# Backward chain: the gradient of the heads' output by 32 rows as weights in four column groups, and dV from it token by token

## Chip, cores and metric

The kernel runs on one core of a Trainium2 chip. The metric is the device time of one execution in microseconds (us). TensorE is the matrix engine: a matmul has a stationary operand (the weights, up to 128x128) and a moving one whose columns stream through; a result with 32 weight columns uses a quarter of the array's columns, and four such column groups can work side by side. VectorE, ScalarE and GpSimd (POOL) copy and calculate; transfers are issued from queues, here those of SyncE (SP) and POOL.

## The reference

A pre-norm block of memory attention followed by a gated FFN, forward and backward. The output and nine gradients are wanted: of x, the start memory, Wq, Wk, Wv, Wo and the three FFN weights.

```python
B, S, Dm = (1, 2048, 448);  H, Dh = (16, 256);  M, seg = (8, 32)
...
mem = mem0
for s in range(n_seg):                      # 64 segments, one after another
    xs = x[:, s * seg_len:(s + 1) * seg_len, :]
    h = concatenate([mem, xs], axis=1)      # 40 rows
    q, k, v = h @ Wq, h @ Wk, h @ Wv        # by head
    p = softmax(where(mask, q @ k.T * scale, -1e9))
    o = (p @ v) @ Wo
    mem = o[:, :M, :]                       # 8 rows to the next segment
    outs.append(o[:, M:, :])
...
h = x + A(layernorm(x));  out = h + swiglu(layernorm(h))
```

The backward pass runs through the segments from 63 to 0. For a segment, with dO the gradient of `o` (40 rows): dOh = dO Wo^T by head, dV = P^T dOh, dP = dOh V^T, dS from the softmax, dQ = dS K, dK = dS^T Q, and the gradient of the 40 input rows is the sum of dV Wv^T, dK Wk^T and dQ Wq^T. Its 8 memory rows belong to dO of the segment before.

## The kernel before

The stages follow one another: the forward chain over 64 segments, the FFN forward and backward over eight pairs of row tiles, the backward chain over 64 segments, then a tail of weight gradients. A tile is four segments (128 rows). All engines' instructions are put in a fixed order when the program is built, by a planner that goes by priorities and its own estimates of durations; what stands in `k.prio.crit()` comes first, in the order of the program text, and other work is put where the planner sees an engine free. `tc.issue_after(x)` puts instructions behind x on their engine. PSUM buffers: `ps1` five, `fx1` two, `po1` one, each a bank of 128 x 2 KB. `evac` copies PSUM to SBUF, on VectorE ("v", L75) or ScalarE ("s", L76).

In SBUF a segment's 40 rows are kept with the 8 memory rows last: columns 0:32 are the segment's own x rows, 32:40 the memory rows. So of the 40 columns the last 32 (`M:L`) hold the 24 output rows and the 8 rows that come from the chain, and the first 8 (`0:M`) hang on no other segment.

One segment s of `backward_chain` (r = s % 4 is its place in its tile t; r goes 3, 2, 1, 0):

- `load_seg` (L1155), for s - 1 while s runs: V from `VG` by a DMA transpose (`load_v`, L1153), Q and K rows from `T1` and `T0q`/`T0k` (L1163, eight loads), all on SP; P from `P_all` on POOL (L1166), from which POOL makes the block-diagonal P_bd of two heads (L1168).
- dOh (L1236): 32 blocks of 128 head columns, each with four parts of the 448 rows of Wo^T; the weights are 128x128 of `WoT_sb`, the 40 columns of `do_roll` are moving: 128 matmuls into four PSUM tiles, copied to `doT` (L75/L76).
- `token_major` (L1245): 16 transposes of `doT` into `dO_sb`, two copies.
- dP (L1254): 32 matmuls of doT and V; then VectorE's chain L1261, L1263, L1264 and L1267, which gives dS_bd.
- `heads("v")` (`head_mm`, L1213): 16 matmuls of dO_sb with P_bd, copied into `blk["v"]` (own rows) and `lo["v"]` (first 8 rows) by ScalarE; `rows_in("v")` (L1293) multiplies 32 rows of each block by Wv^T in four column groups into `pH`.
- `heads("k")`, the turn of dS (L1304, 16 matmuls) with two copies, 12 of K's rows, `heads("q")`, the other 20 of K's rows and 32 of Q's.
- The copy of `pH` to `omb` (L1319), the fp32 matmuls that add the four groups and turn the result (L1322), and VectorE's copy of the 8 memory rows to `do_roll` (L1326), at which the next segment starts.
- At r = 0, not in `crit()`: the first 8 rows of four segments against all three weights (L1378, 96 matmuls), their turn (L1385), the tile's input gradient (L1393) and its layer norm.

`prep_tile` (L1147, L1150) brings 128 rows of the FFN's input gradient `DHb` turned into `do_roll`. The first segment's work is fed by three generator steps inside the last FFN pair, which load Wo^T, Wv^T, Wk^T and Wq^T (3 to 3.6 MB each) where FFN weights lay.

The forward chain has in `qk_rows` (L569, L576) a product in which 32 rows are the weights and 512 columns move, in four column groups, with the last 64 of 448 rows done as two row groups side by side. On SP it stores q and k rows (L824) and V (L826) of each segment.

## Time and profile before

| what | us |
|---|---|
| median of 3 runs | 2935.48 |
| the runs | 2923.96 to 2941.26 |
| the profiled execution | 2921.87 |
| its span | 2920.1 |
| forward chain, about | 40 to 950 |
| FFN, about | 950 to 1257 |
| backward chain | 1257 to 2262 |
| tail | from there to the end |
| TensorE busy in 1281 to 2250 (969 us) | 959.21 |
| VectorE, ScalarE, POOL busy there | 505.20, 372.12, 226.39 |
| share of DMA time there | 0.54 |

In the profile's lines PE is TensorE's matmuls and PEld its weight loads, DVE VectorE, ACT ScalarE; a group is line, engine, operation, output and inputs, shapes, count, busy time, mean duration of one in ns, and idle time before it. The chain of waits gives pieces in order: start, length, engine and line. "issue" is time in which an engine waited for nothing that the profile shows. SPq is SP's queue, with the time that issuing took.

### The profile page before, as it was taken

To read this page: it belongs to the slowest core of one execution; us is meant where nothing else is said; L and a number is where in the kernel's file an instruction comes from. 1 tells how busy PE (TensorE), PEld (TensorE's weight loads), DVE (VectorE), ACT (ScalarE), POOL (GpSimd) and SP (SyncE) were. 2 spreads that over 40 slices of the span, in tenths; PEclk is the share of its full clock that TensorE was granted. 3 is DMA by queue.
4 is the path that set the end of the run, shared out by engine and by line. 5 is a ranking of instruction groups with operands and counts; after the bars stand their busy time and mean duration, and the time that the engine had idled before them with its cause. 6 is when DMAs were issued, how large, how long until landed. Compare 5 with 4: busy or idle time off the path is not lost.

```text
span 2920.1 us, 108265 instructions
## 1 busy us (share of the span) xinstructions
PE 2805.9 (96%) x47650; PEld 1746.3 (60%) x47650; DVE 1328.6 (45%) x3320; ACT 1077.0 (37%) x2590; POOL 704.1 (24%) x1676
## 2 busy tenths in 40 slices
PE   4999999999999999989999999999999989999998
PEld 3555565555555555667777777677766544545444
DVE  4555565556455666745555555555554011111110
ACT  2554454455454454433333333343333011111110
POOL 1222232233222222422222222222222111212211
PEclk9999999999999999999999999999999999999999
DMA  7577777777778988985555555555555998969941
GB/s 258 152 193 192 192 193 195 192 194 200 198 185 229 285 219 215 257 259 151 142 145 154 144 141 155 137 148 149 142 154 170 347 269 175 207 183 238 207 147 52
DMA packets 743132, 552.14 MB, mean 189 GB/s; under 512 B 601796, under 2 KB 639060, under 8 KB 740100
## 3 DMA queue, kind: packets, MB, share of 16 engines
q1 hardware_dynamic: 692788, 402.38, 55.9%
q0 software_dynamic: 49872, 142.83, 14.4%
q8 instruction: 374, 6.13, 0.9%
q14 instruction: 98, 0.80, 0.1%
HBM read 169.84 MB, written 236.13 MB: 139 GB/s over the span
## 4 chain that ended last, share of the span: by engine, by line
PE 80%; issue 8%; DMA 4%; ACT 3%; DVE 2%; POOL 2%; SPq 0%; POOLq 0%; ACTq 0%; DVEq 0%
PE po L1293 11%; PE psf L1487 8%; PE psf L1236 7%; PE psf L569 6%; PE psf L704 5%; PE psf L1213 5%; PE psf L967 4%; PE po L751 4%; PE fx L1378 3%; PE fx L1487 3%; PE fx L1091 3%; PE psf L593 2%; PE psf L1322 2%; PE psf L1245 2%; PE psf L485 2%
## 5 line engine op out<-in xcount | busy, mean ns | idle before, releaser
L76 ACT CAST arA<-psf 128x384 bf16<-128x384 f32 (+6 forms) x1083 | 419.8, 428 | 845.0 <-PE psf L1487 215.1
L75 DVE CAST arA<-psf 128x256 bf16<-128x256 f32 (+6 forms) x797 | 358.4, 471 | 687.8 <-PE psf L1487 248.9
L1293 PE MATMUL po<-arW,arA 128*32 128x448 bf16 x6144 | 328.1, 355 | 5.6 <-DMA arW<-Tq 4.1
L1487 PEld LDWEIGHTS <-arA 128*128 128x128 bf16 x1440 | 139.0, 98 | 160.6 <-issue 4.8
L1236 PEld LDWEIGHTS <-arW 128*128 128x128 bf16 x8192 | 211.2, 96 | 23.3 <-issue 18.4
L1487 PE MATMUL psf<-arW,arA 128*128 128x512 bf16 x882 | 222.7, 381 | 0.0
L1293 PEld LDWEIGHTS <-arA 128*32 128x32 bf16 x6144 | 146.8, 96 | 120.3 <-ACT arA L76 9.3
L1236 PE MATMUL psf<-arA,arW 128*128 128x40 bf16 x8192 | 217.2, 180 | 0.8 <-DVE arA L1326 0.8
L704 PE MATMUL psf<-arW,arA 128*64 128x512 bf16 x1536 | 212.1, 382 | 0.0
L569 PE MATMUL psf<-arW,arA 128*32 128x512 bf16 x3072 | 189.8, 381 | 7.7 <-DVE arA L75 0.9
L76 ACT COPY arA<-psf 128x512 bf16<-128x512 bf16 (+3 forms) x206 | 142.9, 727 | 39.5 <-PE psf L593 24.0
L76 ACT CAST arB<-psf 128x64 bf16<-128x64 f32 (+1 forms) x320 | 107.7, 337 | 135.1 <-PE psf L576 73.6
L967 PE MATMUL psf<-arW 128*128 128x256 bf16 (+1 forms) x1288 | 149.0, 277 | 5.0 <-DVE arA L75 3.7
L75 DVE COPY arA<-psf 128x512 bf16<-128x512 bf16 (+2 forms) x204 | 104.3, 512 | 99.5 <-PE psf L1245 82.4
L967 PEld LDWEIGHTS <-arW 128*128 128x128 bf16 (+1 forms) x1344 | 103.2, 97 | 56.9 <-issue 45.4
L569 PEld LDWEIGHTS <-arA 128*32 128x32 bf16 x3072 | 70.3, 96 | 105.1 <-issue 28.8
L751 PE MATMUL po<-arW,arA 128*32 128x256 bf16 (+1 forms) x4096 | 126.9, 261 | 1.2 <-DVE arA L75 1.2
L1564 POOL DMA_DIRECT2D out_dram<-arA x96 | 52.2, 544 | 262.0 <-DVE arA L75 233.6
L1527 PE MATMUL psf<-arW 128*128 128x448 bf16 x525 | 111.6, 352 | 3.0 <-DVE arA L75 1.6
L1213 PEld LDWEIGHTS <-arW 128*128 128x128 bf16 x2048 | 79.5, 99 | 49.6 <-issue 48.1
L751 PEld LDWEIGHTS <-arA 128*32 128x32 bf16 x4096 | 104.0, 96 | 8.5 <-DVE arA L75 1.5
L1168 POOL COPY arB<-arB 40x320 bf16<-40x320 bf16 x128 | 58.9, 460 | 174.8 <-DMA arB<-P_all 86.7
(298 smaller groups left out, 4553.5 us busy)
## 6 DMA issues: line engine op xcount, KB each, us to landing
arW<-T SPq DMA_DIRECT2D x256, 128.0 KB
X_o<-arA SPq DMA_DIRECT2D x37, 512.0 KB
T<-arA SPq DMA_DIRECT2D x64, 256.0 KB
X_v<-arA POOLq DMA_DIRECT2D x30, 512.0 KB, 4.9
X_k<-arA POOLq DMA_DIRECT2D x30, 512.0 KB, 4.7
X_q<-arA POOLq DMA_DIRECT2D x30, 512.0 KB, 4.1
out_dram<-arA POOLq DMA_DIRECT2D x84, 128.0 KB, 3.8
VG<-arA SPq DMA_DIRECT2D x64, 160.0 KB
```

The lines of the kernel that those rows point to most:

```text
L75: return nc.vector.tensor_copy(out=out, in_=in_)
L76: return nc.scalar.copy(out=out, in_=in_)
L569: nc.tensor.matmul(banks[b][w][32 * q:32 * q + 32, :], lhsT=hT_roll[:, kc, sl, M:L], rhs=(Wq_sb, Wk_sb)[w][:, kc, col(q, b)], start=(b == ...
L704: nc.tensor.matmul(pV[b][64 * g:64 * g + 64, 0:512], lhsT=hT_flat[:, kc, sl * L:sl * L + 64], rhs=Wv_sb[:, kc, n * 512:(n + 1) * 512], sta ...
L751: last = nc.tensor.matmul(pO[32 * q:32 * q + 32, 0:w], lhsT=xblk[:, j, r * SEG:(r + 1) * SEG], rhs=Wo_sb[:, cj(j), 256 * dh:256 * dh + w], ...
L967: nc.tensor.matmul(ps[fp][:, f2 * 256:(f2 + 1) * 256], lhsT=Wt[lo:hi, kc, c * P:(c + 1) * P], rhs=xT[lo:hi, kc, :], start=(kc == 0 and f2 ...
L1091: k.last_dh = nc.tensor.matmul(pdh[:, 0:D], lhsT=srcT[:, tt, c, :], rhs=WT[:, c, :], start=(i == 0), stop=(i == 2 * FC - 1))
L1213: nc.tensor.matmul(ps[b][:, i * 2 * L:(i + 1) * 2 * L], lhsT=lhs[:, at, :], rhs=rhs_bd[:, cl // 2, :, :].rearrange("p g n -> p (g n)"), st ...
L1236: nc.tensor.matmul(pss[b][:, jj * L:(jj + 1) * L], lhsT=WoT_sb[:, kc, c * P:(c + 1) * P], rhs=do_roll[:, kc, sl, :], start=(kc == 0), stop ...
L1293: nc.tensor.matmul(pH[32 * (j % 4):32 * (j % 4) + 32, 0:D], lhsT=blk[nm][:, j, r * SEG:(r + 1) * SEG], rhs=WT[:, cj(j), :], start=(nm == " ...
L1487: k.last_mm = nc.tensor.matmul(pa[i][:, 0:w], lhsT=lhs_of(b)[:, i // 2 * P:(i // 2 + 1) * P], rhs=rhs_of(q, b, i % 2), start=(b == 0), sto ...
L1527: k.last_mm = nc.tensor.matmul(pa[i][:, 0:D], lhsT=lhs_of(b, i), rhs=rhs_of(b), start=(bi == 0), stop=(bi == m + 3))
```

## The change

dOh of a segment is split by rows. The 32 rows `M:L` become the weights: for each part of the 448 rows, four column groups of 32 take four different 1024-column quarters of Wo^T, 512 columns at a time (`grads_by_col`: 12 matmuls for bank 0, eight for the last 64 of the 448 rows in two row groups, 12 for bank 1). The result lies token by token (`dO_own`: partitions are 4 quarters x 32 rows). Four transposes for each bank (`grads_turned`) give the columns `M:L` of `doT` for dP.

The first 8 rows of four segments together are also 32 rows. They are made for the tile t - 1 in two halves in the segments r = 1 and r = 0 of tile t (for the first tile before the chain begins), stored to a new DRAM tensor `RO` by SP, and loaded again segment by segment (`load_rest`); turned, they lie in `R4_b`, from which POOL copies 8 columns into `doT` each segment.

dV is then made from the token-major rows without another transpose: `value_own`, eight matmuls of `dO_own` with P of four heads laid block-diagonally (`P4`, 160 columns), and `value_rest`, eight with 32 weight rows from `dOr` and `P4r`, into the same three PSUM tiles. P4 is loaded by four DMAs on SP (`load_p`), P4r from a new tensor `PR` that the forward chain fills by four stores a segment, after one store of zeros over all of it at s = 0.

The order changes as well: dP begins with the heads whose half is turned; the turn of dS comes before the k heads; all of K's rows come behind the q heads. A pad of 64 columns of `DHb` and `omb` holds a copy of the last 64 columns instead of zeros, since the weights of the last 64 rows lie twice, on both halves of the partitions. Removed are 16 transposes and the 16 head matmuls of dV per segment.

```diff
+              RO=dt("RO", [NT, P, 1024]), PR=dt("PR", [NSEG, 4 * M, 16 * L]),
...
+            blank = A(20, 2560)
+            nc.gpsimd.memset(blank, 0.0)
+            nc.sync.dma_start(out=dr["PR"].rearrange("s q n -> (s q n)").rearrange("(p a n) -> p a n", p=P, n=2560),
+                              in_=blank.unsqueeze(1).to_broadcast([P, 4, 2560]))
...
+        pr = dr["PR"][s].rearrange("(q k) (i c n) -> q k i c n", q=4, i=4, c=4)
+        for q in range(4):
+            g, x = divmod(q, 2)
+            nc.sync.dma_start(out=pr[q, :, :, 2 * x + g, :], in_=P_sb[64 * g:64 * g + M, 4 * x:4 * x + 4, :])
...
+            nc.gpsimd.tensor_copy(out=dh_b[:, D:DP], in_=dh_b[:, D - 64:D])
...
-    WoT_sb = W(0, KC, HD)
+    WoT_sb, Wo3 = W(0, KC - 1, HD), W(24, 2048)
+    dO_own, dOr, P4r = W(28, 2, 512), W(30, 3, P), W(30.75, 4, 4, L)
...
-    dO_sb = A(52, 16, P)
-    doT = A(56, 32, 64)
+    R4_b, hRo = [A(52 + 2 * i, 32, 4 * M) for i in range(2)], B(4.75, KC, 4 * M)
+    doT_flat = A(56, 32 * L + 24)
+    doT = doT_flat[:, 0:32 * L].rearrange("p (c n) -> p c n", n=L)
+    P4 = A(58.5625, 4, 4, L)
...
+        nc.gpsimd.tensor_copy(out=hRo.rearrange("p k (g j) -> p k g j", j=M), in_=do_roll[:, :, s0:s0 + 4, 0:M])
+
+    def grads_by_col(lhs, banks, part, alone=False):
+        last = None
+        if part in ("h", "h0", "h1"):
+            for q in range(4):
+                for b in (0, 1) if part == "h" else (int(part[1]),):
+                    nc.tensor.matmul(banks[b][32 * q:32 * q + 32, :], lhsT=lhs(KC - 1)[64 * b:64 * b + 64], rhs=Wo3[64 * b:64 * b + 64, 512 * q:512 * q + 512],
+                                     start=(part == "h" and b == 1), stop=(part != "h" or b == 0), skip_group_check=True)
+        else:
+            for kc in range(KC - 1):
+                for q in range(4):
+                    c0 = 1024 * q + 512 * part
+                    last = nc.tensor.matmul(banks[part][32 * q:32 * q + 32, :], lhsT=lhs(kc), rhs=WoT_sb[:, kc, c0:c0 + 512],
+                                            start=(kc == 0 and (part == 0 or alone)), stop=(part == 1 and not alone and kc == KC - 2), skip_group_check=True)
+        return last
+
+    def grads_out(banks, b):
+        k.evac(dO_own[:, b, :], banks[b][:], "vs"[b])
+
+    def grads_turned(pt, dst, b):
+        for i in range(4):
+            last = nc.tensor.transpose(pt[:, 512 * b + i * P:512 * b + (i + 1) * P], dO_own[:, b, i * P:(i + 1) * P], ident[:, :])
+        k.evac(dst.rearrange("p (x c) n -> p x c n", x=2)[:, :, 8 * b:8 * b + 8, :],
+               pt[:, 512 * b:512 * b + 512].rearrange("p (c x n) -> p x c n", x=2, n=32), "v")
+        return last
+
+    def rest_rows_saved(t, b):
+        nc.sync.dma_start(out=dr["RO"][t][:, 512 * b:512 * b + 512], in_=dO_own[:, b, :])
+
+    def load_rest(s):
+        t, r = divmod(s, 4)
+        src = dr["RO"][t].rearrange("(q r k) (m e) -> r q k m e", q=4, k=M, e=P)
+        for w in range(3):
+            n = (3, 3, 2)[w]
+            nc.sync.dma_start(out=dOr[32 * w:32 * w + 32, 0:n], in_=src[r][:, :, 3 * w:3 * w + n])
+            nc.sync.dma_start(out=P4r[32 * w:32 * w + 32].rearrange("p i c n -> p (i c n)"), in_=dr["PR"][s])
+
+    def load_p(s):
+        pa = dr["P_all"][s].rearrange("p (x i n) -> p x i n", x=2, n=L)
+        for q in range(4):
+            g, x = divmod(q, 2)
+            nc.sync.dma_start(out=P4[32 * q:32 * q + 32, :, 2 * x + g, :], in_=pa[64 * g + M:64 * g + L, x])
 
     def load_v(s):
         return nc.sync.dma_start_transpose(out=vT, in_=dr["VG"][s])
 
     def load_seg(s):
+        load_p(s)
         if s < NSEG - 1:
+            load_rest(s)
             load_v(s)
...
+    def rest_lhs(kc):
+        return hRo[:, kc, :]
+    with k.prio.crit():
+        banks = [k.ps1(), k.ps1()]
+        for part in (0, "h", 1):
+            grads_by_col(rest_lhs, banks, part)
+        pt = k.ps1()[:].bitcast(BF16)
+        for b in range(2):
+            grads_out(banks, b)
+            grads_turned(pt, R4_b[(NT - 1) % 2], b)
+            rest_rows_saved(NT - 1, b)
+        load_rest(NSEG - 1)
...
+    def v_bank(ps, b):
+        n = (3, 3, 2)[b]
+        return 3 * b, n, ps[b][:, 0:4 * L * n]
+
+    def v_out(ps, m):
+        return v_bank(ps, m // 3)[2].rearrange("p (x m n) -> p x m n", x=2, n=2 * L)[:, :, m % 3]
+
+    def p_rows(rhs, m):
+        return rhs[:, m // 2].rearrange("p (x g) n -> p x (g n)", x=2)
+
+    def value_rest(ps):
+        for m in (0, 3, 6, 1, 4, 7, 2, 5):
+            w, a = divmod(m, 3)
+            nc.tensor.matmul(v_out(ps, m), lhsT=dOr[32 * w:32 * w + 32, a, :], rhs=p_rows(P4r[32 * w:32 * w + 32], m),
+                             start=(a == 0), stop=False, skip_group_check=True)
+
+    def value_own(ps, m0, m1):
+        for m in range(m0, m1):
+            nc.tensor.matmul(v_out(ps, m), lhsT=dO_own[:, m // 4, m % 4 * P:(m % 4 + 1) * P], rhs=p_rows(P4, m),
+                             start=False, stop=True, skip_group_check=True)
+
+    def v_rows(ps, b):
+        m0, n, bank = v_bank(ps, b)
+        return slice(2 * m0, 2 * m0 + 2 * n), bank.rearrange("p (x c n) -> p x c n", x=2, n=L)
...
-            pss = [k.ps1() for _ in range(4)]
-            for j in range(MC):
-                c = cj(j)
-                b, jj = divmod(j, 8)
-                for kc in range(KC):
-                    with tc.issue_after(k.last_dh.ins) if s == NSEG - 1 and j == 0 and kc == 0 else nullcontext():
-                        nc.tensor.matmul(pss[b][:, jj * L:(jj + 1) * L], lhsT=WoT_sb[:, kc, c * P:(c + 1) * P],
-                                         rhs=do_roll[:, kc, sl, :], start=(kc == 0), stop=(kc == KC - 1))
-            for b in range(4):
-                k.evac(doT[:, 8 * b:8 * b + 8, 0:L], pss[b][:, 0:8 * L].rearrange("p (c n) -> p c n", n=L), "vsvs"[b])
-
-            def token_major(hf):
-                ph = k.ps1()[:].bitcast(BF16)
-                for i in range(8):
-                    c0 = 2 * (8 * hf + i)
-                    nc.tensor.transpose(ph[:, i * P:(i + 1) * P], doT[:, c0:c0 + 2, :].rearrange("p c n -> p (c n)"), ident[:, :])
-                k.evac(dO_sb[:, 8 * hf:8 * hf + 8, :], ph.rearrange("p (c n) -> p c n", n=P), "sv"[hf])
-            token_major(0)
-            token_major(1)
+            def own_lhs(kc):
+                return do_roll[:, kc, sl, M:L]
+            banks = [k.ps1(), k.ps1()]
+            for part in (0, "h", 1):
+                with tc.issue_after(k.last_dh.ins) if s == NSEG - 1 and part == 0 else nullcontext():
+                    grads_by_col(own_lhs, banks, part)
+            grads_out(banks, 0)
+            grads_out(banks, 1)
+            nc.gpsimd.tensor_copy(out=doT[:, :, 0:M], in_=R4_b[t % 2][:, :, r * M:(r + 1) * M])
+            pV = [k.ps1() for _ in range(3)]
+            value_rest(pV)
+            pt = k.ps1()[:].bitcast(BF16)
+            grads_turned(pt, doT[:, :, M:L], 0)
+            value_own(pV, 0, 4)
+            grads_turned(pt, doT[:, :, M:L], 1)
             pD = k.ps1()
-            for h in range(8):
-                for g in range(2):
-                    for dc in range(DC):
-                        j = 2 * (2 * h + dc) + g
-                        nc.tensor.matmul(pD[64 * g:64 * g + 64, h * L:(h + 1) * L], lhsT=doT[:, j, :], rhs=vT[:, 2 * h + dc, L * g:L * g + L],
-                                         start=(dc == 0), stop=(dc == DC - 1), skip_group_check=True)
+            ready = [(0, 0), (0, 1), (1, 0), (4, 0), (4, 1), (5, 0), (1, 1), (5, 1)]
+            for h, g in ready + [(h, g) for h in (2, 3, 6, 7) for g in range(2)]:
+                for dc in range(DC):
+                    j = 2 * (2 * h + dc) + g
+                    last_d = nc.tensor.matmul(pD[64 * g:64 * g + 64, h * L:(h + 1) * L], lhsT=doT_flat[:, j * L:j * L + 64], rhs=vT[:, 2 * h + dc, L * g:L * g + L],
+                                              start=(dc == 0), stop=(dc == DC - 1), skip_group_check=True)
+            with tc.issue_after(last_d.ins):
+                value_own(pV, 4, 8)
...
-            heads("v", dO_sb, P_bd)
+            def rows_in(nm, WT, js):
+                for j in js:
+                    last = nc.tensor.matmul(pH[32 * (j % 4):32 * (j % 4) + 32, 0:D], lhsT=blk[nm][:, j, r * SEG:(r + 1) * SEG],
+                                            rhs=WT[:, cj(j), :], start=(nm == "v" and j < 4), stop=(nm == "q" and j >= MC - 4),
+                                            skip_group_check=True)
+                return last
+            for b in range(3):
+                js, v = v_rows(pV, b)
+                k.evac(blk["v"].rearrange("p (x c) n -> p x c n", x=2)[:, :, js, r * SEG:(r + 1) * SEG], v[:, :, :, M:L], "s")
+            if s == 0:
+                k.tl.outs(7, 9, 0, 6)
             score_grads()
-            first_rows("v")
-            rows_in("v", WvT_sb, 0, MC)
-            heads("k", Q_sb, dS_bd)
+            for b in range(3):
+                js, v = v_rows(pV, b)
+                k.evac(lo["v"].rearrange("p (x c) n -> p x c n", x=2)[:, :, js, r * M:(r + 1) * M], v[:, :, :, 0:M], "s")
+            with tc.issue_after(last_d.ins):
+                last_v = rows_in("v", WvT_sb, [16 * x + j for a, e in ((0, 6), (6, 12), (12, 16)) for x in range(2) for j in range(a, e)])
+            if r < 2 and t > 0:
+                rest_bank = [k.ps1()] * 2
+                with tc.issue_after(last_v.ins):
+                    for part in ((1, "h1") if r == 0 else (0, "h0")):
+                        grads_by_col(rest_lhs, rest_bank, part, True)
             pT = [k.ps1(), k.ps1()]
             for h in range(8):
                 for g in range(2):
...
             for g in range(2):
                 turned["vs"[g]] = k.evac(dST_bd[64 * g:64 * g + L, :, g, :],
                                          pT[g][64 * g:64 * g + L, 0:8 * L].rearrange("p (h n) -> p h n", n=L), "vs"[g])
+            with tc.issue_after(last_t.ins):
+                heads("k", Q_sb, dS_bd)
+            if r < 2 and t > 0:
+                with tc.issue_after(turned["sv"[r]].ins):
+                    grads_out(rest_bank, 1 - r)
+                rest_rows_saved(t - 1, 1 - r)
             with tc.issue_after(turned["v"].ins):
                 own_rows("k", 2, "v")
             first_rows("k", turned)
-            with tc.issue_after(last_t.ins):
-                rows_in("k", WkT_sb, 0, 12)
-            heads("q", K_sb, dST_bd)
-            rows_in("k", WkT_sb, 12, MC)
-            rows_in("q", WqT_sb, 0, MC)
+            last_q = heads("q", K_sb, dST_bd)
+            with tc.issue_after(last_q.ins):
+                rows_in("k", WkT_sb, range(MC))
+            if r < 2 and t > 0:
+                grads_turned(k.ps1()[:].bitcast(BF16), R4_b[(t - 1) % 2], 1 - r)
+            rows_in("q", WqT_sb, range(MC))
             first_rows("q", turned)
             k.last_om = nc.vector.tensor_copy(out=om[:, 0:D], in_=pH[:, 0:D])
+            nc.vector.tensor_copy(out=om[:, D:DP], in_=pH[:, D - 64:D])
```

## The prediction

> **What bounds the kernel now.** I read the page first (busy shares, slices, the chain's shares), then the chain of waits and the timeline of single segments of the backward chain, then the same for the forward chain and the hand-over. From the page:

> ```profile
> span 2920.1 us, 108265 instructions
> PE 2805.9 (96%) x47650; PEld 1746.3 (60%) x47650; DVE 1328.6 (45%) x3320; ACT 1077.0 (37%) x2590; POOL 704.1 (24%) x1676
> PE 80%; issue 8%; DMA 4%; ACT 3%; DVE 2%; POOL 2%; SPq 0%; POOLq 0%; ACTq 0%; DVEq 0%
> L1236 PE MATMUL psf<-arA,arW 128*128 128x40 bf16 x8192 | 217.2, 180 | 0.8 <-DVE arA L1326 0.8
> ```

> TensorE is busy nearly everywhere, so what counts is how long it issues, and where a serial chain holds it. The output gradient by head is L1236, 128 matmuls a segment. One ordinary segment in the chain of waits (start, length, what):

> ```profile
> 1618.03 3.30 PE psf L1236 x128
> 1621.33 1.00 PE psf L1245 x16
> 1622.33 0.62 PE psf L1254 x32
> 1622.95 0.74 PE psf L1213 x16
> 1623.69 0.30 PE fx L1378 x4
> 1624.00 1.60 PE po L1293 x32
> 1625.60 0.01 issue
> 1625.61 0.73 PE psf L1213 x16
> 1626.35 0.30 PE psf L1304 x16
> 1626.65 0.74 PE po L1293 x12
> 1627.39 0.68 PE psf L1213 x16
> 1628.07 2.57 PE po L1293 x52
> 1630.64 0.75 PE fx L1378 x13
> 1631.39 1.06 PE psf L1322 x8
> 1632.45 0.49 PE fx L1378 x6
> ```

> The segment takes 14.91 us and TensorE never rests. L1378 (first rows of the last tile) is filler put where TensorE would wait: for the VectorE chain behind dP (1623.00 to 1625.61), and for the copies around the fp32 turn L1322. Three segments of a tile take 14.9; the one that also has L1385 and L1393 takes 17.2 (1571.05 to 1588.25). Sixteen tiles at (3 x 14.9 + 17.2) = 61.9 us are the 980 us of the backward chain.

> The price of the new form is in the forward chain, where 32 rows are already weights in column groups:

> ```profile
> 705.78 1.48 PE psf L569 x24
> 707.26 0.56 PE psf L576 x16
> 707.82 1.41 PE psf L569 x24
> ```

> **The change, part by part.**

> *From the start of a segment to dP.* Before: 3.30 + 1.00 + 0.62, and VectorE starts on dP 4.97 us after the segment began. After: part 0 is 12 matmuls of 512 columns, 12/24 of 1.41 = 0.71; the halves are 8, 0.28 to 0.34 (half of 0.56, with 0.05 for the change of form); part 1 another 0.71. The sum is 1.76, and L569's single time of 0.38 against 0.06 per issue leaves about 0.17 of tail. Bank 0 is copied by VectorE (128x512 CAST, 0.69) under part 1. Bank 1 is copied by ScalarE (128x512 CAST, 0.59): 1.76 + 0.17 + 0.03 + 0.59 + 0.03 = 2.58. Its four transposes take 0.23 + 0.16 (L593, x4: 0.39), giving 2.97; VectorE's copy of 128x512 bf16 0.42 + 0.06, giving 3.45; the second half of L1254 0.31 + 0.17, giving 3.95. In the 0.82 us while bank 1 is copied TensorE does the rest-row products, four transposes (0.23) and four own products of 160 columns (0.28 by L666's two in 0.17). The eight rest-row products have 32 weight rows each, a form that the trace doesn't have: 0.2 us if the three row groups run at once, 0.8 if they run singly at L666's 0.085 and a change of form. I take 0.4, as the row nearest in kind, L576 with two row groups, did overlap. That is 0.1 more than is covered: 4.05 us, a gain of 0.92 per segment.

> *The VectorE chain.* Its 2.61 us stay. Under it lay 0.74 + 0.30 + 1.60; now 0.28 of own products and the value rows at 1.60 + 0.14. ScalarE's six value copies took 1.54 together and keep that length; the row order begins with bank 0, so little waits. Some 0.6 us is left open in segments r = 2 and 3, for filler. In r = 0 and 1 the half for the next tile's rest rows stands there: 12 + 4 matmuls, 0.71 + 0.28 = 1.0, 0.4 over.

> *From the k heads to the row copy.* 5.08 us before. The same matmuls in another order (turn, k heads, q heads, 64 rows): 0.30 + 0.73 + 0.68 + 3.2 + 0.14, equal. But 12 rows no longer lie between the k and the q heads, and five PSUM buffers must serve two turned, three k and three q tiles: the last q tile waits for a copied k tile. By the copies' lengths (0.48 after 0.42 on ScalarE, then the 0.24 first rows) that costs about 0.2. In r = 0 and 1 the rest bank holds one of the five until its copy (0.59 or 0.69, behind the turned copy) is done: about 0.5 in all, and 0.25 of transposes. The second small copy of the row gradient (128x64, 0.21) hides behind six of the eight 0.13 us turns of L1322; if not, 0.2 a segment.

> *Sum per tile.* r = 2 and 3: -0.92 + 0.2 = -0.7 each. r = 0 and 1: -0.92 + 0.4 + 0.5 + 0.25 = +0.2 each. The 2.3 us by which one segment is longer is serial L1385/L1393 work; with wider gaps elsewhere for L1378 I give it back 1.0. Total -2.0 us, 16 tiles: -33 us. Bounds: counting TensorE's issue alone, 4 x (3.30 + 1.00 + 0.74) = 20.2 goes and 4 x (1.76 + 0.40 + 0.46 + 0.56) + 2 x 1.25 = 15.2 comes: -80 us if no wait shows. If the rest products run singly, all waits show and nothing fills: +0.6 a tile, +10 us.

> The trace prices a change between forms of the array itself: 12 rows of L1293 took 0.74 where 52 took 2.57, so 0.15 more than their share; L569 shows 0.05. [...]

> *DMAs, backward.* Ten more loads per segment (four of P, three pairs for the rest rows) on SP, all single-buffered. SP issues one transpose of 1.3 to 1.6 and eight loads at 0.3 to 0.4 in an ordinary segment, about 4 of 14.9 us, 7 in the longest; ten more at 0.33 make 7 to 10. The P load waits for the last own products (4.4 us in) and is wanted 16 us in; the T loads queued behind would land some 4 us later, 14 us in, and are wanted by the k heads 21 us in. In r = 0 the rest rows go out and back through memory before the next segment's rest products: store issued 9 us in, landed 11.5 (stores on POOL land in 3 to 5 us, so up to 14), reload 14.5 to 17, wanted at 16.6: 0 to 1 us per tile, within the bounds. Packets: queue 1 took 55.9% of 16 engines' 2920 us for 692,788 packets, 38 ns each; about 700 more per segment is 1.7 us of 14.9, so DMA goes from 0.54 to some 0.65. Nothing.

> *POOL.* The copy of 8 rows into doT (like L834, 0.40) is ready once the old dP is done, and POOL idles 11 of 15 us; 0. It could stand behind the P_bd copies that wait for P_all, which would still end before the segment does.

> *Hand-over.* L1236 starts at 1257.6 but the segment ends at 1281, since Tq lands at 1275 with DMA full from 1200 to 1280. The last tile's rest rows (28 matmuls, 2 us) are stored and reloaded in that crowd; if the reload lands behind Tq at 1276, 12 us of segment follow and it costs 8; if before, nothing, and POOL's blank of the row tile (VectorE waited 1.1 for it) goes. I take +3.

> *Forward.* Four stores of 8 partitions per segment on SP, 0.35 to 0.7 each: SP issued 6.8 us of 13.7, so they fit. The blank of 2.6 MB is issued once; from 60 to 80 us DMA was 0.15 to 0.19 busy, so it hides, but SP ran without pause from 79 to 117 and the rest-row weights (L832, 96.5) come five us ahead of L485: 0 to +8, I take +2.

> All: -33 + 3 + 2 = -28 us. Against the profiled execution (2921.87, span 2920.1) that is 2894. The median of the three runs is 0.5% higher, 2935.48, and there it gives 2907; I say 2905. About 0.5% (15 us) is what a measurement of this kernel tells from no change.

> **The rivals.**
> 1. *The floor is reached* (0.15): the planner fills every gap with L1378 and TensorE's issue is all; -50 to -80, 2855 to 2885. For it: 96% busy today. Against: two or three new copy-and-return waits in a row before dP.
> 2. *The gain goes into waits* (0.17): the r = 0 and 1 segments lose what the others win through PSUM buffers; -14 to +14, 2921 to 2950. For it: five buffers, more tiles alive at once.
> 3. *SP's queue becomes the bound* (0.18, slower): loads issued behind a transpose took 1.25 to 1.30 here. With about 5 us of other issue, ten loads pass today's 15.5 us mean from 1.05 us each; at 1.3 a segment is 18 us, +160. Nearer to it, at 1.1 to 1.15, +30 to +60. Against: most such loads take 0.33, and the transpose is one a segment.

> **How the numbers follow.** Forecast, 2886 to 2920: 0.50. So faster 0.50 + 0.15 = 0.65, same 0.17, slower 0.18. The range 2862 to 2955 takes in most of rivals 1 and 2 and the small end of 3. The likeliest case's own range is 2886 to 2920.

> **What would show it.** Right: segments of r = 2 near 14.2 us, those of r = 0 and 1 near 15.1, VectorE's first operation on dP 4.0 to 4.1 us after the segment's start, L569-like own matmuls at 1.8 us. Wrong: SP issuing without a pause, or the rest-row products waiting for a DMA; the q heads waiting for k copies by more than 0.5 us; rest products at 0.8 us; the first segment ending later than 10 us after Tq lands.

## The result and the profile after

The changed kernel takes 3113.01 us (median of 4 runs, 3103.74 to 3129.22) against 2934.89 for the kernel before in the same session: a ratio of 1.062, 95% interval 1.056 to 1.067. The prediction was 2905 us, between 2862 and 2955. It was wrong in sign and in range. The page of the changed kernel:

```profile
span 3108.2 us, 97474 instructions
PE 2837.1 (91%) x41634; PEld 1639.3 (53%) x41634; DVE 1349.6 (43%) x3432; ACT 1001.1 (32%) x2478; POOL 734.8 (24%) x1770
PE 67%; issue 8%; DMA 8%; DVE 6%; ACT 4%; SPq 4%; POOL 2%; POOLq 0%; ACTq 0%; DVEq 0%
L1175 PE MATMUL psf<-arW,arA 128*32 128x512 bf16 x1536 | 108.6, 387 | 9.4 <-DVE arA L1440 9.4
```

There are 6000 matmuls less, but TensorE's busy time has not fallen (2806 before). Its share of the ending chain fell from 80% to 67%; DMA, VectorE and SP's queue took that share. The profiled execution is 3109.94 us, its span 188 us longer than before's. The places, from the first and last instruction of each stage in the two timelines: the forward chain ends 12 us later, the middle phase's last product (L1098) 12 more, the first row copy of the backward chain comes another 14.5 later, the 62 segments between the first and the last row copy take 1110.0 us instead of 956.3, and what follows is 4.5 shorter.

So the backward chain is the main part. I time a segment from one copy of the memory rows (L1440, before L1326) to the next; medians by place r in the tile:

| kernel | us | r=3 | r=2 | r=1 | r=0 | chain | clock lost |
|---|---|---|---|---|---|---|---|
| before | 2935 | 17.30 | 14.78 | 14.88 | 14.91 | 956 | 3 |
| changed | 3113 | 15.95 | 18.35 | 15.53 | 21.87 | 1110 | 60 |

"Chain" is the time from the first to the last row copy. "Clock lost" is the sum of one minus the granted clock over its single microseconds, in us. One r=1 segment and the r=0 segment behind it, from the chain of waits of the changed kernel (start, length, what):

```profile
1698.76 0.83 PE psf L1175 x12
...
1701.37 0.44 DVE arA L75
1701.85 0.40 PE psf L1184 x4
...
1707.66 0.60 DVE arW L75
1708.26 0.34 DVE arA L75
1708.63 0.05 issue
1708.68 0.58 SPq L1463
...
1710.38 1.29 SPq L1204
...
1712.67 0.65 SPq L1197
...
1716.17 3.77 DMA arA<-VG
1719.94 0.14 issue
1720.07 0.69 PE psf L1345 x31
...
1725.35 0.34 SPq L1190
1725.73 2.18 DMA arW<-T0k
1727.91 0.09 issue
1728.00 0.73 PE psf L1282 x16
1728.73 3.11 PE po L1387 x28
```

Read it from the end back. The q heads at 1728.00 waited for a K row load (T0k), issued at 1725.73, right behind the store of the rest rows (L1190). dP at 1720.07 waited for V (VG), issued only at 1716.17 behind ten new loads (L1204, L1197, L1198) and two older ones (L1463), and all of these stood behind another L1190 that waited for the rest rows' copy at 1707.66. SP's own waits over the chain say the same (waiting instruction, what for: us, times, longest):

```profile
SPq L1204 <- PE psf L1304: 126.4, 33, 6.5
SPq L1190 <- DVE arA L75: 120.5, 15, 9.9
SPq L1190 <- ACT arW L76: 77.2, 15, 7.5
```

The store waits 15 times in r=1 and 15 times in r=0, 6.6 us on average, with the next segment's V, K and Q rows queued behind it. The last line of the chain shows the second effect: 28 products took 3.11 us, where 32 of the same kind took 1.63 four us later. The granted clock (the third number from the end) in and behind TensorE's wait:

```profile
1724.00:1728.00 4.00, 1.01 (x31) 0.77 (x24) 1.62 (x5) 1.53 (x4) 0.91 (x2) 1.00 0.66 232
1728.60:1731.80 3.20, 3.20 (x37) 1.12 (x34) 0.99 (x4) 0.62 (x2) 0.55 (x1) 0.51 0.31 84
```

After a stretch in which TensorE was busy for a quarter of the time, the next 3.4 us ran at half clock. The changed chain has 28 such stretches of 3.4 or 6.8 us, the old one 2, both in its first 35 us.

### The profile page after: what moved, and what is told of

Same layout as the page of the kernel before. It is cut to its first block, busy times and chain, and to the rows that moved or that the text cites. A ratio compares the mean times of both kernels' runs of the same rounds, so it can differ in the third digit from the quotient of the medians.

```text
span 3108.2 us, 97474 instructions
## 1 busy us (share of the span) xinstructions
PE 2837.1 (91%) x41634; PEld 1639.3 (53%) x41634; DVE 1349.6 (43%) x3432; ACT 1001.1 (32%) x2478; POOL 734.8 (24%) x1770
## 3 DMA queue, kind: packets, MB, share of 16 engines
q0 software_dynamic: 49872, 142.83, 13.7%
## 4 chain that ended last, share of the span: by engine, by line
PE 67%; issue 8%; DMA 8%; DVE 6%; ACT 4%; SPq 4%; POOL 2%; POOLq 0%; ACTq 0%; DVEq 0%
PE psf L1601 8%; PE po L1387 8%; PE psf L570 5%; PE psf L705 4%; PE po L752 4%; PE psf L1175 3%; PE fx L1098 3%; PE psf L974 3%; PE fx L1492 3%; PE fx L1601 3%; PE psf L594 2%; PE psf L1282 2%; DMA arA<-VG 2%; PE psf L1436 2%; ACT arA L76 2%
## 5 line engine op out<-in xcount | busy, mean ns | idle before, releaser
L76 ACT CAST arA<-psf 128x96 bf16<-128x96 f32 (+3 forms) x955 | 364.6, 422 | 771.7 <-PE psf L1601 215.1
L75 DVE CAST arA<-psf 128x256 bf16<-128x256 f32 (+5 forms) x669 | 292.7, 465 | 560.1 <-PE psf L1601 249.9
L1387 PE MATMUL po<-arW,arA 128*32 128x448 bf16 x6144 | 359.6, 379 | 3.9 <-DVE arA L75 3.9
L1387 PEld LDWEIGHTS <-arA 128*32 128x32 bf16 x6144 | 175.2, 101 | 132.3 <-issue 32.9
L75 DVE COPY arA<-psf 128x512 bf16<-128x512 bf16 (+2 forms) x300 | 128.0, 427 | 181.3 <-PE psf L1184 163.6
L570 PE MATMUL psf<-arW,arA 128*32 128x512 bf16 x3072 | 191.1, 383 | 7.7 <-DVE arA L75 0.9
L76 ACT CAST arW<-psf 128x512 bf16<-128x512 f32 x204 | 116.4, 587 | 152.1 <-PE psf L1175 108.6
L1282 PE MATMUL psf<-arB,arW 128*128 128x80 bf16 x2048 | 112.7, 210 | 46.1 <-DMA arW<-T0k 42.5
L570 PEld LDWEIGHTS <-arA 128*32 128x32 bf16 x3072 | 70.5, 96 | 106.1 <-issue 29.9
L1282 PEld LDWEIGHTS <-arW 128*128 128x128 bf16 x2048 | 91.9, 104 | 63.5 <-issue 47.0
L75 DVE CAST arW<-psf 128x512 bf16<-128x512 f32 x116 | 79.9, 689 | 103.0 <-PE psf L1169 80.1
L1175 PE MATMUL psf<-arW,arA 128*32 128x512 bf16 x1536 | 108.6, 387 | 9.4 <-DVE arA L1440 9.4
L752 PEld LDWEIGHTS <-arA 128*32 128x32 bf16 x4096 | 103.9, 96 | 8.6 <-DVE arA L75 1.5
```

What stands on the lines that cost most here:

```text
L75: return nc.vector.tensor_copy(out=out, in_=in_)
L76: return nc.scalar.copy(out=out, in_=in_)
L570: nc.tensor.matmul(banks[b][w][32 * q:32 * q + 32, :], lhsT=hT_roll[:, kc, sl, M:L], rhs=(Wq_sb, Wk_sb)[w][:, kc, col(q, b)], start=(b == ...
L752: last = nc.tensor.matmul(pO[32 * q:32 * q + 32, 0:w], lhsT=xblk[:, j, r * SEG:(r + 1) * SEG], rhs=Wo_sb[:, cj(j), 256 * dh:256 * dh + w], ...
L1175: last = nc.tensor.matmul(banks[part][32 * q:32 * q + 32, :], lhsT=lhs(kc), rhs=WoT_sb[:, kc, c0:c0 + 512], start=(kc == 0 and (part == 0 ...
L1282: last = nc.tensor.matmul(ps[b][:, i * 2 * L:(i + 1) * 2 * L], lhsT=lhs[:, at, :], rhs=rhs_bd[:, cl // 2, :, :].rearrange("p g n -> p (g n ...
```

## The experiments

All times are beside runs of the kernel before on the same chip, which took 2926 to 2935 us. The versions build on each other, so I give one table (kernel time, segment medians, chain, clock lost, all in us), and then each with its edit.

| kernel | us | r=3 | r=2 | r=1 | r=0 | chain | clock lost |
|---|---|---|---|---|---|---|---|
| e1: store on POOL | 3038 | 16.52 | 18.92 | 15.53 | 15.63 | 1039 | 32 |
| e2: V and K first | 3347 | 25.18 | 18.11 | 21.45 | 20.85 | 1322 | 196 |
| e3: no trip | 3117 | 15.95 | 18.60 | 15.53 | 22.05 | 1117 | 60 |
| e4: two banks | 3135 | 15.66 | 18.25 | 15.13 | 23.13 | 1130 | 96 |
| e5: e1 and e4 | 3029 | 16.80 | 18.32 | 15.13 | 15.23 | 1034 | 34 |
| e6: waits filled | 3042 | 16.71 | 18.96 | 15.13 | 15.23 | 1044 | 26 |
| e7: stages before | 3010 | 16.04 | 18.03 | 15.13 | 15.23 | 1019 | 29 |
| e8: e5, no first rows | 2971 | 16.86 | 13.85 | 15.13 | 15.23 | 964 | 36 |
| e9: before, no first rows | 2930 | 16.15 | 14.73 | 15.63 | 14.75 | 951 | 52 |
| e10: first rows spread | 2977 | 14.04 | 14.34 | 15.65 | 20.00 | 984 | 22 |
| e11: turn moved | 2977 | 15.64 | 15.41 | 15.87 | 16.11 | 982 | 15 |
| e12: before, turn moved | 2934 | 17.30 | 14.78 | 14.88 | 14.90 | 958 | 4 |
| e13: rest rows last | 2974 | 17.19 | 14.23 | 16.05 | 16.11 | 990 | 26 |
| e14: e1, rest rows last | 3105 | 25.22 | 14.23 | 15.53 | 15.63 | 1095 | 70 |
| e15: V, then rest rows | 2966 | 14.47 | 14.75 | 15.87 | 16.11 | 974 | 16 |

### Is it the store, the trip, or the shared tile? (e1 to e4)

The edit of e1:

```diff
-        nc.sync.dma_start(out=dr["RO"][t][:, 512 * b:512 * b + 512], in_=dO_own[:, b, :])
+        nc.gpsimd.dma_start(out=dr["RO"][t][:, 512 * b:512 * b + 512], in_=dO_own[:, b, :])
```

> The stores of the rest rows' gradients (two per token tile) are issued by POOL instead of SP; nothing else is changed. Theory one (SP issues in program order, so a store that waits for its PSUM copy holds the K and V loads queued behind it): the r=0 segment falls from 21.9 us to 16-17, r=2 stays near 18, the kernel takes 3000-3030 us. Theory two (the ten additional loads per segment are simply too much for SP, whatever else stands in the queue): r=0 stays above 20 us and the kernel within 10 us of 3113. Theory three (TensorE's clock halves after idle time and is the larger part): if r=0 loses its idle time the half-clock windows in the backward chain fall from 28 to under 12.

The edit of e2, in `load_seg` (`last_load` is the last K or Q load):

```diff
-        load_p(s)
         if s < NSEG - 1:
-            load_rest(s)
             load_v(s)
...
+        with tc.issue_after(k.last_load.ins):
+            load_p(s)
+            if s < NSEG - 1:
+                load_rest(s)
```

> On SP each segment's V and K/Q loads are issued first and the ten additional loads (P by head, rest rows, their P) behind them; the stores stay on SP. Theory one: the order in SP's queue is what counts; r=0 gets V in time and falls to 17-19 us, but the additional loads now come late, and the rest products wait for them: about +1 us in r=1 and r=2; the kernel takes 3020-3060 us. Theory two (volume): no order helps, 3100 us or more.

The edit of e3 (RS is a tensor that nothing loads, RO is filled with zeros once in the forward chain):

```diff
-        nc.sync.dma_start(out=dr["RO"][t][:, 512 * b:512 * b + 512], in_=dO_own[:, b, :])
+        nc.sync.dma_start(out=dr["RS"][t][:, 512 * b:512 * b + 512], in_=dO_own[:, b, :])
```

> The rest rows' gradients are stored to another DRAM tensor, and the loads read one that was blanked at the start: the loads wait for no store (the rest rows' share of dV is left out, the work is the same). The stores keep their place in SP's queue. If what costs is the wait of the store in SP's queue, r=0 stays near 21 us and only the start of the backward chain gets shorter, by 10-20 us, so that the kernel takes 3090-3105 us. If it is the trip through DRAM (store lands, then the load may start), r=0 falls to 16-17 us and the kernel to under 3020 us.

The edit of e4 (within `grads_turned` both halves then use columns 0 to 511 of their tile):

```diff
-            grads_turned(pt, doT[:, :, M:L], 1)
+            grads_turned(k.ps1()[:].bitcast(BF16), doT[:, :, M:L], 1)
```

> The two halves' transposes write a PSUM tile each, so that the second half's need not wait for VectorE's copy of the first. If the shared tile costs what the r=1 segment of the trace shows (0.45-0.5 us between ScalarE's copy and the first transpose of the second half), every segment gets 0.4-0.5 us shorter and the kernel 20-30 us: 3083-3093 us, r=1 at 15.0-15.1. If that wait lies beside a DMA's wait in r=0 and r=2, only r=1 and r=3 gain: 3097-3107 us.

e1 took 3037.74 us (ratio 1.037, interval 1.034 to 1.040): one queue's name is worth 75 us. r=0 fell from 21.87 to 15.63, further than theory one said, with all ten loads still there: their number was not what held r=0. The total stayed 8 us above theory one's range. SP's long waits are now those of the loads of P for TensorE's last own products, and those for the store's landing ahead of the loads of RO (the longest, 18.4, lies in the hand-over ahead of the chain). From e1's waits of SP:

```profile
SPq L1204 <- PE psf L1304: 161.9, 51, 6.1
SPq L1197 <- DMA RO<-arW: 78.4, 16, 18.4
```

The half-clock stretches fell from 28 to 19, not to under 12: the store's wait is not the only thing that brings them.

e3 (3117.05) leaves the store's wait where it is and takes the trip away: r=0 stayed at 22.05. What holds r=0 is the store's wait in the queue, not the trip. The 10 to 20 us expected at the start of the chain did come: SP issued the loads of RO for the first segment at 1264 to 1267, ahead of the end of the middle phase, no wait for RO is left there, and from the last product of the middle phase to the first row copy it takes 27.4 us instead of 40.4. The kernel is no faster for it: its middle phase ended 9 us later (the forward chain alone 13, at 955 instead of 942), and the second segment takes 19.1 us instead of 14.2, since its loads of RO and PR issued only from 1309 on, as SP stood in its order behind the weights (Tk, Tq), a transpose, and the loads of P. The edit need not be to blame for the forward chain: e1, which does not touch it, ended it at 955 too, so its length differs that much between executions of nearly the same work.

e2 was a bad miss: 3346.64, where I expected 3020 to 3060. The K and Q loads wait for the heads of the running segment, so everything placed behind them is late in every segment, and the clock lost rises from 60 to 196 us. TensorE's waits in e2's chain, on the rest products (L1301) and on the transposes behind:

```profile
PE psf L1301 <- DMA arW<-PR: 91.3, 85, 3.1
PE psf L1184 <- DVE arA L75: 59.3, 62, 2.5
```

The lesson is the same from the other side: on this queue, the loads had to stand in the order in which their buffers come free.

e4 (3134.83, interval of the ratio 1.067 to 1.073) is slower than the changed kernel, though r=1 and r=3 fell by 0.40 and 0.29 as expected (the total was to be 3107 at most). The store holds r=0's loads as before, and the clock is lower. The granted clock over the chain (third number from the end), first of the changed kernel, then of e4:

```profile
1320.00:2430.00 1110.00, 971.19 (x17100) 579.80 (x17100) 518.47 (x1328) 294.98 (x943) 250.68 (x636) 0.95 0.54 139
```

```profile
1323.00:2454.00 1131.00, 986.26 (x17107) 587.28 (x17106) 518.98 (x1329) 296.18 (x943) 250.86 (x639) 0.92 0.54 137
```

There are 36 half-clock stretches instead of 28. That a shorter segment came with a slower kernel is measured; that the lower clock is the whole reason is argued from these two lines.

### Both edits, and the waits filled (e5, e6)

> Both edits together: the rest rows' stores on POOL and a PSUM tile for each half's transposes. If the second tile alone was slower only because a shorter r=1 segment came sooner to the store that held SP (r=0 grew by 1.3 us while r=1 and r=3 fell by 0.4 and 0.3), then with the store off SP every segment keeps its 0.3-0.4 us: r=0 15.2, r=1 15.1, r=2 18.5, r=3 16.2, the backward chain 1010-1018 us instead of 1039, the kernel 3010-3018 us. If the second tile costs something of its own (more half-clock windows, a PSUM buffer missing elsewhere), the kernel stays at 3030-3050 us.

e5 has no edit beyond those of e1 and e4. The edit of e6, which is also made three times ahead of L1499 and twice ahead of L1507:

```diff
+    def fill_wait(bank, n):
+        for _ in range(n):
+            nc.tensor.matmul(bank[0:32, 0:D], lhsT=ident[:, 0:32], rhs=WqT_sb[:, 0, :], start=True, stop=True)
...
+            with tc.issue_after(last_w.ins):
+                fill_wait(pm, 3)
```

> As the kernel with both edits, with additional matmuls that compute nothing: three of 448 columns in each segment where TensorE waits for the row copy before the fp32 turn, and three and two per tile where it waits between the last tile's first-row products, their turn and their transposes. Their results are overwritten. They add about 64 x 0.56 + 16 x 0.9 = 50 us of TensorE work, nearly all of it in waits of 0.3 to 1.0 us. If the clock halves because of those short waits, the clock lost in the backward chain falls from some 30 us to under 10 and the kernel is 15-25 us faster than without them, although it does more. If the short waits do not matter to the clock, it is 0 to 20 us slower.

e5 (3028.88) has r=0 and r=1 at 15.23 and 15.13, as expected, so with the store off SP the second tile keeps its 0.4 us. The total missed (3010 to 3018 expected): r=3 is uneven as in e1, 15.7 to 17.7 us in nine tiles and 19 to 21.5 in six, with waits for V.

e6 put 272 empty products at TensorE's waits, 67 us of its busy time where 50 were estimated. Clock loss went from 34 to 26 us, not under 10, and the kernel became 13 us slower (3041.72). Those short waits are not the main source of the half clock; the theory for that run fell.

### The stages ahead of the chain (e7)

```diff
-            nc.sync.dma_start(out=pr[q, :, :, 2 * x + g, :], in_=P_sb[64 * g:64 * g + M, 4 * x:4 * x + 4, :])
+            nc.gpsimd.dma_start(out=pr[q, :, :, 2 * x + g, :], in_=P_sb[64 * g:64 * g + M, 4 * x:4 * x + 4, :])
...
-    nc.sync.dma_start(out=WqT_sb, in_=dr["Tq"])
...
         load_rest(NSEG - 1)
+    nc.sync.dma_start(out=WqT_sb, in_=dr["Tq"])
```

> As the kernel with both edits, and: the forward chain's four stores of P per segment go to POOL instead of SP, and Tq, the last weight load before the backward chain, is issued behind the first rest rows' loads instead of ahead of them. If SP's 2.8 us per forward segment push the transposes at every 16th segment back and with them POOL and the memory rows that TensorE waits for (10-17 us where it was 3), the forward chain ends near 942-946 us instead of 954-968; the hand-over (last product of the middle phase to the first row copy) falls from 35-40 us to 27-31. Together 18-30 us less than without these two edits: 2985-2997 us. If POOL is the bottleneck of those segments, the forward chain gets longer instead, by 1-2 us per segment at most.

e7 took 3010.34 us (two runs, 3000 and 3021, so that its gain of 18 on e5 is no larger than their difference). The forward chain's 64 segments differ between the kernels mainly in three places, the 17th, 33rd and 49th, where rows of 16 segments are turned by DMA. Before, these were 3.0, 2.5 and 2.2 us longer than the ordinary 13.4; in the changed kernel 12.4, 4.1 and 3.0; in e3 17.0, 12.8 and 3.4; in e7 3.1, 3.2 and 7.0. They differ between executions too: e1 has the changed kernel's forward chain, and there they were 12.6, 10.0 and 8.8. POOL's timeline in the first of them, in the changed kernel:

```profile
269.31 1.00 POOL L501 COPY arA<-arW 128x128 bf16<-128x128 bf16 x4
285.02 0.55 POOL L546 DMA_DIRECT2D X_o<-arA  x1 [14.71 <-DMA arA<-arA]
```

A store of POOL waits 14.71 us for a transpose that SP issued late (278.3, before 271.3), as four stores of P (2.8 us) now stand ahead of it; before, the wait was 8.10. The copy of memory rows that TensorE needs (L818) comes behind that store, and TensorE waits 7.0 us for it (before 0.8). The hand-over, from the last L1098 to the first row copy, fell only to 34.8 us (before 25.9, changed 40.4), not to 27-31. In the changed kernel TensorE waited 14.3 us in it for one load of RO:

```profile
PE psf L1299 <- DMA arW<-RO: 17.1, 3, 14.3
```

In e7 the longest such wait was 10.9.

### What the new segment takes by itself (e8, e9)

In both, 92 of the 96 products of a tile's first rows are left out; they are the filler that is put into TensorE's gaps.

```diff
-                for j in range(MC):
+                for j in range(4 if wi == 0 else 0):
```

> The kernel with both edits, with 92 of the 96 products of the last tile's first rows (L1492) left out, so that hardly any filler stands in the backward chain. It measures the new segment bare. The one segment of the trace that had no filler, the first whole one, took 14.2 us with a shared tile and 13.8 with two. If that holds, r=3 falls from 15.7-16.8 to 13.8-14.0 us, r=0 and r=1 stay at 15.1-15.2, r=2 keeps the serial work on the last tile's rows and takes 16.5-17.5; sum 61 us a tile, chain 970-985 us, kernel 2965-2980. If r=3 stays above 15 us, filler was not what made it longer than the 14.2 us of the prediction.

> The kernel before with the same 92 products per tile left out (L1378): the old segment bare, to be set against the new one. If the old segment's filler lay in TensorE's waits, an ordinary segment stays at 14.6-14.9 us and the new form's 13.8 in r=2 and r=3 is a real gain of 0.9, as predicted. If TensorE's own work set the old segment's length, its 23 fillers of 0.054 us come off: 13.7-14.0 us, and the new form is no shorter in r=2 and r=3 and 1.2 us longer in r=0 and r=1. The kernel takes 2915-2935 us in the first case and 2855-2885 in the second.

e8's r=2 segment is the new segment bare, 13.85 us. One of them, timeline lines of TensorE and VectorE:

```profile
1647.00 0.83 PE L1175 MATMUL psf<-arW,arA 128*32 128x512 bf16 x12 [0.28 <-DVE arA L1440]
1648.10 0.83 PE L1175 MATMUL psf<-arW,arA 128*32 128x512 bf16 x12
1651.16 0.49 DVE L1354 SCALAR_TENSOR_TENSOR prod<-psf,arB 128x320 f32<-128x320 f32 x1 [0.62 <-PE psf L1345]
1653.68 0.38 PE L1410 MATMUL psf<-ident,arB 128*40 128x40 bf16 x16 [0.43 <-DVE arB L1360]
1658.79 0.62 DVE L1432 COPY omb<-po 128x448 f32<-128x448 f32 x1 [2.04 <-PE po L1387]
1660.59 0.19 DVE L1440 CAST arA<-psf 128x32 bf16<-128x32 f32 x1 [1.04 <-PE psf L1436]
```

Own matmuls to dP 4.16 us, VectorE's chain 2.52, turn to row copy 5.11. In the old kernel the bare segment stays at 14.73 (r=2; 14.78 with filler): there the filler lay in waits and cost next to nothing. So the new form does save 0.9 us in r=2, and in r=3 where neither serial work nor a product between its heads stands (13.83 in five tiles of e10, below), and is 0.4 to 0.5 us longer than 14.73 in r=0 and r=1: some -0.9 us a tile. e8's total, 2971.22, is where I expected it, but r=2 was not the segment that kept the serial work: the order changed, and it went to r=3.

The whole kernel e9 takes 2929.53 us (ratio 0.9996, interval 0.997 to 1.002), but that is a gain and a loss in one. With the filler gone, its chain had 30 half-clock stretches and 52 us of clock lost, where before had 2 and 3, and this cost time. Two of its r=1 segments, with the same 344 matmuls, the first at full clock and the second with a half-clock stretch (windows, then the first 128 products of each from the chain of waits):

```profile
1366.30:1381.00 14.70, 13.47 (x344) 10.07 (x344) 7.53 (x18) 5.51 (x17) 3.17 (x9) 1.00 0.50 154
1426.70:1442.20 15.50, 14.26 (x344) 10.96 (x344) 7.48 (x18) 5.51 (x17) 3.17 (x9) 0.89 0.47 137
1366.57 3.35 PE psf L1236 x128
1426.90 4.16 PE psf L1236 x128
```

From row copy to row copy the first takes 14.72 us and the second 15.59; r=1 has such a stretch in all but two tiles. r=3, which has one in all tiles but one, fell from 17.30 to 16.15 even so, and the two nearly cancel. So the filler had a use in the old kernel: it kept the clock up.

### Where the filler stands (e10 to e15)

In the changed kernel 28 of the 96 products stood between the k and the q heads of r=3, and in r=2 the serial work that follows them (copy, fp32 turn L1499, two copies, transposes L1507), which put 3.0 to 3.4 us between the heads. The order on each engine is laid down ahead of time from estimated durations, so I moved them by hand.

The edit of e10, on e7, in the segments r=3, r=2 and r=1 (a third of the products in each, the serial work in the last):

```diff
+        with tc.issue_after(last_q.ins):
+            for fn in spread_px.pop(s, []):
+                fn()
```

> The kernel of the previous round with stores on POOL, two tiles, and the later Tq, in which the 96 products of a tile's first rows are let go in three parts, behind the q heads of the next tile's r=3, r=2 and r=1 segments, and the serial work behind them after r=1's: 25 to 36 stand in each segment in the order built, none between the k and the q heads of r=3. If the lump of 28 between the heads and its companions are what makes r=3 and r=2 1.5-2 us longer than bare, r=3 and r=2 fall to 14.2-14.8 us, r=1 grows to 15.3-15.7, r=0 takes the serial work and grows to 18-18.5; sum of the four 62.5-63.5 us against 64.4-66, the chain 985-1000 us, the kernel 2965-2985. If the serial work costs more next to the rest rows' half, r=0 is over 19 and nothing is gained.

e10 took 2976.64 us (e7: 3010). r=3 and r=2 became 14.04 and 14.34, as expected; r=0, which got the serial work, takes 18.5 or 20.0, in every second tile the longer, where a half-clock stretch falls into it. TensorE's waits in it:

```profile
PE fx L1513 <- ACT om L1509: 11.0, 14, 0.8
PE fx L1521 <- ACT arB L1517: 4.6, 14, 0.3
```

e11 lets the products go a segment earlier, and puts the fp32 turn into r=1's wait for the row copy (`last_w` is the last row product) and the transposes behind r=1's own turn (`last_m`). e12 does the same in the kernel before.

```diff
+            if r == 1:
+                work[0](last_w)
...
+        if r == 1 and work is not None:
+            work[1](last_m)
```

> As the last version, with the first rows' products released a segment earlier (done by r=1's heads), their fp32 turn put into the wait for the row copy at the end of r=1 and their four transposes behind r=1's own turn, so that no product waits between the heads; the loads of the tile's rows move from r=1 to the next tile's r=3, and the first rest rows' P is loaded ahead of the weights. If the serial work was dear (3.3 to 4.9 us in r=0) because it waited in front of the q heads, and the clock halved behind it, r=0 falls to 15.2-15.6, r=1 grows to 16.5-17, r=2 and r=3 stay at 14.0-14.4; sum 60.5-61.5, the chain 950-968 us, the kernel 2930-2955. If the half clock comes in any case or the vector work of the layer norm delays the next segment, r=0 or r=1 stays over 18 us and the kernel over 2965.

> The same move of the first rows' products, turn and transposes in the kernel before, nothing else. Its r=3 segment holds the serial work today (17.3 us against 14.9). If the move is what helps, and not the new form, the kernel before gains as well: r=3 falls to 14.9, one other segment grows by 1.0-1.3 us, 1.1-1.4 us a tile, 2906-2918 us, and it stays ahead of the changed kernel in every version. If its waits at the turn are already full of filler, nothing is gained: 2925-2940.

In e11 r=0 and r=1 took 16.11 and 15.87, in sum as expected (r=0 longer and r=1 shorter than I had said) and 3.7 us less than e10's, but r=3 and r=2 became uneven, 14.3 to 17.9, with 17 waits for V (31 us), and the chain began 14 us later than e10's: 2977.09 where 2930 to 2955 was expected, a ratio of 1.017 (1.013 to 1.020). The early load of the first rest rows' P also changes e11's values; the later versions do without it. In e12 the move did not take: r=3 still has 17.30, the kernel 2933.56, so it says nothing on whether the old kernel would gain.

The order of SP's loads in e13 (on e11) and e14 (on e1), in `load_seg` (with `ro` it loads the rest rows, with `pr` their P); the lines left out are the K and Q rows:

```diff
+        if s < NSEG - 1:
+            load_v(s)
         load_p(s)
         if s < NSEG - 1:
-            load_rest(s)
-            load_v(s)
+            load_rest(s, ro=s % 4 != 3)
...
+        if s < NSEG - 1 and s % 4 == 3:
+            with tc.issue_after(k.last_load.ins):
+                load_rest(s, pr=False)
```

> As the last version (first rows' products released early, their turn in the wait at the end of r=1), with the first rest rows' P loaded where it was, and another order on SP: V and P by head first, the rest rows' P next, the K and Q rows, and in r=3, the segment whose rest rows have just been stored, the loads of those rows last. If the waits for V in r=3 and r=2 (17 waits, 31 us, each followed by slower segments) come from V's load standing behind a load that waits for the store's landing, they go: r=3 14.3, r=2 14.3-14.5, r=1 15.9, r=0 16.1, the chain 955-965 us, the kernel 2945-2960. If SP is simply full in those segments, V or the rest rows stay late and r=3 and r=2 stay at 15.5 or more on average.

> The changed kernel with the stores on POOL (the first experiment) and this order on SP, nothing else. The first experiment's r=3 segments were uneven: 15.9 to 17.0, with 19.7-20.4 three times, and r=0 and r=1 up to 16.9. If a load that waits for the store's landing ahead of V made them so, r=3 becomes 15.9-16.5 throughout, the chain falls from 1039 to 1018-1026 us and the kernel from 3038 to 3012-3025. If SP is full, no change, 3030 or more.

And in e15 (on e11), which also issues the first store of rest rows from SP:

```diff
+        if s < NSEG - 1:
+            load_v(s)
         load_p(s)
         if s < NSEG - 1:
             load_rest(s)
-            load_v(s)
```

> As the version with first rows' products released early and stores on POOL, with SP's order: V, P by head, rest rows with their P, then K and Q rows, in every segment, and the last tile's rest rows (the first ones saved) stored from SP, which is idle there, instead of from POOL behind the middle phase's stores. If the order alone made r=3 and r=2 uneven, V comes in time now as in the last runs and the rest rows are 3 us less late in r=3: r=3 14.3-14.8, r=2 14.2-14.3, r=1 15.9-16.1, r=0 16.1, the chain 956-966 us, the hand-over 27-30 us, the kernel 2925-2948, level with the kernel before within what a measurement can tell. If r=3 stays over 16 us because SP is full, 2955-2970.

With V first, r=2 is 14.2 us in nearly every tile but the first, in e13 and e14 alike: the order theory, for V. Putting the rest rows' loads last was wrong, and e13's total, 2973.80, missed the 2945 to 2960 expected. In e13 the rest products of r=3 wait for them:

```profile
PE psf L1306 <- DMA arW<-RO: 19.1, 20, 2.1
```

In e14 something else happened: 75 products of the first rows and all their serial work with the layer norm were put into r=3's wait on TensorE and VectorE, and the segment took 25.2 us. That the order was laid down so because these loads were estimated late is my reading; no run shows it. I had expected 3012 to 3025; it took 3104.62.

e15 has r=3 at 14.47, but now r=2 is uneven (14.3 or less in eight tiles, 15.2 to 19.7 in the others), waiting for the rest rows' P:

```profile
PE psf L1301 <- DMA arW<-PR: 21.3, 15, 2.5
```

In that place the queue also holds the transposes of the next tile's rows and the three loads moved there. e15 takes 2966.21 us where 2925 to 2948 was expected, a ratio of 1.013 (1.011 to 1.015): the best version, still 35 us behind the kernel before. In its profile the first row copy comes 27 us later than before's, and the chain is 17 longer. Its hand-over is 42 us, where I expected 27 to 30: the store landed early, but Tk and Tq were issued ahead of the loads that wait for it, and one of these kept TensorE waiting for 15.2 us. No version beat the old kernel. Whether SP could serve all segments in another order, or is too full where a tile begins, stays open.

## Why the prediction was wrong

Four segments were to take 61.9 - 2.0 = 59.9 us a tile, and their medians add up to 71.7. The steps that failed are, by size, "DMAs, backward ... Nothing" (6.2 us a tile), "I give it back 1.0" for the serial work (4.6), and the four transposes of bank 1 (0.4 a segment; in r=3 and r=2 it lies within the 4.6). Together they are 11.6 of the 11.8. What the chain lost besides is ahead of it, in the forward chain, the middle phase and the hand-over. In the prediction's order:

- *From the start to dP: 4.05 us said, 4.55 measured* (1698.76 to VectorE's first operation on dP at 1703.31). Most terms held: own matmuls 1.93 with their tail (1.76 + 0.17), rest products 0.31 (0.4 taken, 0.2 to 0.8 given), and 4.16 in all with two tiles. The term that failed is "its four transposes ... giving 2.97": they did not start at 2.58, when ScalarE's copy was done, but at 3.09, behind VectorE's copy of the other half, since both halves write one PSUM tile. e4 and e5 show it: with a tile each, 0.3 to 0.4 us a segment where no load is waited for.
- *Changes of form,* at an estimate of 0.15 us each from the trace (12 rows of L1293 took 0.74 where 52 took 2.57), were not added to the sum for the new segment. With two tiles the whole phase from the start to dP is 0.11 over my sum (4.16 against 4.05), less than one of them; no run takes their share apart.
- *The VectorE chain and the rows:* 2.61 kept, 2.52 measured bare; the rest half 0.4 over, 0.47 measured; 5.28 from k heads to row copy, 5.11 in r=2; 5.83 in r=1, 5.95 measured. These held.
- *The sum for four segments without the serial work* (-0.7, -0.7, +0.2, +0.2: -1.0 a tile) was right for the form with two tiles, -0.9, with some luck: r=3 and r=2 gain 0.2 more each than said, r=0 and r=1 lose 0.2 more each. As built, the shared tile takes 1.6 of it back.
- *"With wider gaps elsewhere for L1378 I give it back 1.0": wrong by 4.6 us a tile.* r=3 and r=2 together should have been 2 x 14.2 + 1.3 = 29.7 and were 34.3. The order built put 28 products and the serial work in front of the q heads. e8's r=2 (13.85) and e10's r=3 and r=2 (14.04, 14.34) show it: without that work they are near 14. e10 keeps only part of this, since the serial work then lengthens its r=0 by 3.3 to 4.8 us; e11, where it stands in waits, has 16.11 and 15.87 in r=0 and r=1, 0.9 and 0.7 over the bare ones. The old kernel had its 23 products a segment in waits; that cover, more than the serial work's length, was what I should have followed.
- *"DMAs, backward ... Nothing": the largest error, 6.2 us a tile.* I costed the store by when it lands and the loads by their issue times, which were right (medians of 0.31 to 0.63 us by kind of load, transposes aside, far from rival 3's 1.05). I named the T loads behind P's loads, but not what is queued behind the store's own wait on SP: the next segment's V and K. e1 (one queue's name, 75 us) and e3 (no trip, and r=0 as long) settle it. Rival 3 came true by another road: SP idle and blocked, not SP full. What SP held back was V (12 us of TensorE's waits in the chain) and the K rows (42 us, of which T0k is the last to land).
- *Forward +2 (0 to 8): 12.* SP's mean share (6.8 of 13.7 us) hid that three segments already had SP's transposes in POOL's way. The 12 is one execution's; e1 and e5, with the same forward chain, ended it 26 and 20 us later than before. *Hand-over +3 (0 to 8): 14.5,* by the mechanism named, the reload behind Tq (14.3 us of wait), but dearer; without the trip (e3) it was 1.5.
- *The clock was in no term.* I treated a wait as its own length; behind the longer waits of r=0 and r=2 TensorE then ran at half clock. Segments at the same place in one run, with one 3.4 us stretch of half clock and without, differ by 0.7 us (changed, r=2: 19.07 and 18.34), 1.1 (e1, r=1: 16.65 and 15.53) and 1.5 (e10, r=0: 20.00 and 18.51). An estimate from these for the 35 windows of 3.4 us in the changed chain is 25 to 50 of the 154 us that it grew by. No run kept the waits and took the half clock away, so this share lies within the points above and is not shown apart from them.
- The middle phase's 12 us are not explained; in other versions it was 1 to 8 us longer than before.
- Slips that decide nothing: 16 tiles of -2.0 are -32, not -33; 16 times 61.9 is 990, not 980; and 0.38 less 0.06 is 0.32, not the tail of 0.17, though own matmuls and tail then took the 1.93 of the sum.
